# Two loads moved to a later place, x's differences on VectorE, and a front that begins two places later with its halves closer

## The chip, the cores and the metric

The kernel runs on one core of a Trainium2 chip. Its time is the device time of one launch, in microseconds (us), the median of three runs. A core has a matrix engine (TensorE, PE in the profile; its weight loads are PEld), VectorE (DVE), ScalarE (ACT), GpSimd (POOL) and SyncE (SP). Each engine works through its own instructions in order. SP only issues transfers (DMA) between the chip's memory (HBM) and the core's on-chip buffer, and it stands still at a transfer whose target is not yet free; ACT issues some transfers too.

## The reference

For each of 8 batches (8 heads, 576 positions, 64 channels a head), linear attention, then a perceptron on the normed rows, then an expert layer that needs the result:

```
q_s = softmax(q over channels);  k_s = softmax(k over positions)
x   = q_s @ (k_s^T @ v)                       # heads side by side: 576 x 512
xn  = (x - mean(x)) / sqrt(var(x) + 1e-6) * g_ln
x   = x + relu(xn @ w_ch1) @ w_ch2            # 512 -> 2048 -> 512
out = sum over each row's 2 best of 4 experts of weight * (causal attention of the expert)(x)
```

All numbers are float32. The kernel splits an operand into a high and a low part for the matrix engine and multiplies three of the four combinations, so each product is three matmuls.

## The kernel before, in words

The work of this case lies in the first half of the program, which makes x of every batch and runs 12 of the 16 column blocks of the perceptron (the rest and the experts come after about 760 us).

**Fronts.** `front(b)` is all that makes batch b ready for its perceptron: four *units* (`a_unit`, one for each pair of heads; unit n is pair n % 4 of batch n // 4), then the norm of the two halves of 288 rows (`layer_norm`), then the differences (`Mix`). A unit takes its k and q from tiles loaded for it; in its fourth piece it issues the loads of k and q for unit n + 2 (`load_qk(next_unit(n))`), and in its sixth those of v (`load_v`). The pools have two buffers, so unit n + 2 takes the buffers of unit n, and its load on SP waits until unit n has read them.

**Differences.** From batch 2 (`FAST`) on, the first product of the perceptron is done by a scheme with 7 products in place of 8: x's four quarters b11, b12, b21, b22 (column half, row half) and four differences t1 to t4 of them, each 128 x 576. `Mix.less` makes a difference; `Mix.part` splits a quarter or a difference into high and low (ACT, then DVE, the helper on lines 201 and 202). In the trace the differences are line 777 (`sq<-xc` is t1, `sq<-xc,sq` t2, `xc<-xc` t3, `xc<-xc,sq` t4), the split quarters `xm` and `xw_b`, the split differences `xw_a`.

**Rounds.** Batches 2 to 7 have a round each, `fast_pieces(b)`. A round is a list of TensorE pieces, by groups: 7 products of 2 x 6 matmuls (`fast_group`; they write banks pa, pb, pc), then 8 sums of 12 matmuls (`second`; acc), each of which DVE adds to x (L1418) before its bank is used again. The weights of a product come as one 512 KB tile `w_r`, streamed from HBM into five tiles in turn (`Stream`): the load of tile n is issued in the program right after product n - 5 has freed it. The fifth of the five exists only from `last_space` on, which stands after the first pieces of batch 2's round.

**Places.** `run_pieces` divides a round's matmuls into 44 places (`END`) and puts the steps of the next batch's front between them: unit pr begins at place 4 * pr (`UNIT_GAP`), the norm's halves `NORM_GAP` places apart, the differences behind. All of it is moved forward by `EARLY` places, so that a front's first steps fall into the round before. Batch 2's own front has no such move; it lies in the last pass of the simple method.

**What sets the order.** Program order decides on SP. On the other engines a scheduler reorders within the program's dependences by a timeline of its own, so a changed place also moves instructions around it. The order below is read from the built programs.

Of the kernel before, what the change touches and what calls it, by code (L numbers as in the profile page):

```python
# [12 lines left out]
ALU = mybir.AluOpType  # L13
# [27 lines left out]


UNIT_AT, UNIT_GAP = (0, 1, 2, 4, 5, 7), 4
NORM_AT, NORM_GAP = (0, 2, 4, 6, 8, 10), 8

REBASE = 2.0 ** -112

# [3 lines left out]
FAST = 2  # L51
# [89 lines left out]
def tile_kernel(ctx: ExitStack, tc: tile.TileContext, q, k, v, g_ln, w1, w2, w_gate, wq, wk, wv, wo, out):  # L141
    nc = tc.nc
# [5 lines left out]
    NPR = H // 2  # L148
# [48 lines left out]
    def pool(name, bufs=1, **kw):  # L197
        return tc.tile_pool(name=name, bufs=bufs, reuse_waits="tile", **kw)
# [34 lines left out]
    def x_hl(pl, name):  # L233
        return pl.tile([P, 2, NDC, T], F32R, tag="big", name=name)


    class Wide:
# [7 lines left out]
        def load(self):  # L245
            n = len(self.tiles)
            if n < len(self.blocks):
                r = self.pool_r.tile([P, DM, 2], I32, tag="r", name="wraw")
                src = self.blocks[n][0]
                dst = r.rearrange("p f t -> p (f t)")  # L250
                if len(src.shape) == 3:
                    dst = dst.rearrange("p (c f) -> p c f", c=src.shape[1])
                nc.sync.dma_start(out=dst, in_=src)
                self.tiles.append(r)
# [70 lines left out]
    def fc_tiles(pl, f, w=None):  # L325
        w1s[f] = pl.tile([P, 2, NDC, P], F32R, tag=f"w1_{f}", name=f"w1_{f}") if w is None else w
        w2s[f] = pl.tile([P, 2, DM], F32R, tag=f"w2_{f}", name=f"w2_{f}")
        return fc_blocks(f, w1s[f], w2s[f])
# [54 lines left out]
    def unit_buf(n):  # L383
        return n if n < NPR else n % 2

    def next_unit(n):

        return n + NPR if n < 2 else n + 2 if n >= NPR else len(units)
# [4 lines left out]
    def load_qk(n):  # L393
        for nm in "kq":
            load(n, nm)
# [13 lines left out]
    def load_v(n):  # L409
        if n >= len(units):  # L410
            return
        b, pr = units[n]
        t = vbuf[unit_buf(n)]
        base = v[b, 2 * pr]
        rows = lambda first, dims: bass.AP(tensor=base.tensor, offset=base.offset + first * D, ap=dims)
        for j in range(2):
            nc.sync.dma_start(out=t[:CS, :NIL, j, :D],
                              in_=rows(j * S, [[NIL * D, CS], [D, NIL], [1, D]]))
        nc.sync.dma_start(out=t[:, NIL, :, :D],
                          in_=rows(S - P, [[D, P], [S * D, 2], [1, D]]))  # L420
# [184 lines left out]
    def a_unit(n):  # L605

        u = Heads(n)
        for piece in (u.k_rows, u.q_max, u.q_below):
            piece()
        yield  # L610
        for piece in (u.k_turn, u.k_max, u.q_exp):
            piece()
        yield
        for piece in (u.k_spread, u.k_below, u.k_exp, u.q_sum, u.q_more, u.q_one, lambda: u.q_scale(0), lambda: u.q_scale(1)):
            piece()
        yield
        if next_unit(n) >= 2 * NPR:
            load_qk(next_unit(n))
        u.q_turn()
        for piece in u.q_parts(0):  # L620
            piece()
        yield
        u.kv_product()
        for piece in u.q_parts(1):
            piece()
        u.kv_sums()
        for j in range(2):
            u.kv_high(j)
            u.kv_low(j)
        yield  # L630
        if next_unit(n) >= 2 * NPR:
            load_v(next_unit(n))
        for h in range(NH):
            u.result(h)
            u.keep(h)
        yield
# [5 lines left out]
    class Norm:  # L642
# [40 lines left out]
        def less(self, c, n):  # L683
            if c == 0:
                self.xc = lp.tile([P, NDC, T], F32, tag="xc", name="xc", bufs=2)
            nc.vector.tensor_tensor(self.xc[:, c:c + n], self.xs[:, c:c + n],
                                    self.pmu[:, None].to_broadcast([P, n, T]), op=ALU.subtract)
# [75 lines left out]
    class Mix:  # L763
# [10 lines left out]
                self.at["t1"], self.at["t2"] = u.sq[:, :2], u.sq[:, 2:]  # L774

        def less(self, o, x, y):
            nc.gpsimd.tensor_tensor(self.at[o], self.at[x], self.at[y], op=ALU.subtract)

        def early(self):
            self.less("t1", "b12", "b11")  # L780
# [120 lines left out]
    def calls(fn):  # L901
        while True:
            fn()
            yield
# [11 lines left out]
    def load_wqk(s, r):  # L916
        def fill(t):
            for j in range(2):
                nc.sync.dma_start(out=t[:, :, j * D:(j + 1) * D],
                                  in_=(wq, wk)[s][2 * r + j].rearrange("(c p) d -> p c d", p=P))  # L920
        w = wqk[s, r] = mid.tile([P, 2, NDC, P], F32R, tag="r", name="wqk")
        load_moe(hp, fill, w[:, 0], w[:, 1])

    def load_wv(r):
        def fill(t):
            for j in range(2):
                nc.sync.dma_start(out=t[:, :, j * D:(j + 1) * D],
                                  in_=wv[2 * r + j].rearrange("(c p) d -> p c d", p=P))
        w = moe["vg"]
        load_moe(hp, fill, *(w[:, i, :, r * P:(r + 1) * P] for i in (0, 1)))  # L930
# [336 lines left out]
    def cut(t, at, shape):  # L1267
        n = 1
        for d in shape[1:]:
            n *= d  # L1270
        t = t[:, at:at + n]
        if len(shape) == 4:
            t = t.rearrange("p (a b c) -> p a b c", a=shape[1], b=shape[2])
        elif len(shape) == 5:
            t = t.rearrange("p (a b c d) -> p a b c d", a=shape[1], b=shape[2], c=shape[3])
        else:
            t = t.rearrange("p (a b) -> p a b", a=shape[1])
        return t
# [190 lines left out]
    def once(fn):  # L1469
        fn()  # L1470
        yield
# [9 lines left out]
        yield  # L1481

    late = ExitStack()
    END, EARLY = 44, 4

    def front(b):
        slots = front_slots(b)
        mixes[b] = m = Mix(b)
        add = lambda n, fn: slots.setdefault(n, []).append(once(fn))
        t = max(slots) + 1  # L1490
        add(t, m.early)
        if b == FAST:
            for i, nm in enumerate(("b11", "b21")):
                add(t - 6 + i, lambda nm=nm: m.part(nm))
            add(t + 2, m.fourth)
            add(t + 2, m.send)
            add(48, lambda: x_pair(("b12", "b22")))
            for i, nm in enumerate(("b12", "b22", "t1", "t2", "t3")):
                add(49 + i, lambda nm=nm: m.part(nm))
        else:  # L1500
            add(t + 0.5, lambda: m.part("b12"))
            for i, nm in enumerate(XMADE):
                add(t + 1 + i / 2, lambda nm=nm: m.part(nm))
            add(t + 4.5, m.send)
            slots = {n - EARLY: gs for n, gs in slots.items()}
        return slots

    slots = front(FAST)
    fronts = {FAST + 1: front(FAST + 1)}
    def begin(b, slots, end):  # L1510

        for n in [n for n in fronts.get(b, ()) if n < 0]:
            slots.setdefault(end + n, []).extend(fronts[b].pop(n))
# [21 lines left out]
    for b in range(FAST, B):  # L1535
        if b < LAST:
            slots, n = fronts.pop(b + 1), END
            if b + 2 < B:
                fronts[b + 2] = front(b + 2)
                begin(b + 2, slots, n)  # L1540
        else:
            slots, n = {}, 4 * NFC
            p1r.close()
            x2s_last[0] = t = x_hl(xtp, "x2")
            t = t.rearrange("p a b c -> p (a b c)")
            stream.use(before_last + 7, before_last + 7 * NG, [cut(t, 8 * P * i, WSL) for i in range(2)] + ring[MIDB:] +
                       [later[2].tile(WSL, F32R, tag="qT", name="w_r")])
            wcp = late.enter_context(pool("w_c", side="right"))
            moe["vg"] = wcp.tile([P, 2, NDC, VG], F32R, name="wvg")
            blocks = []  # L1550
            for f in range(FSPLIT, NFC):
                blocks += fc_tiles(wcp, f)
            wide = Wide(blocks, mid, hp, AHEAD)
            conv = calls(wide.step)
            todo = [conv] * len(blocks)
            for s in range(2):
                for r in range(NR):
                    todo.append(calls(lambda s=s, r=r: load_wqk(s, r)))
            for r in range(NR):
                todo.append(calls(lambda r=r: load_wv(r)))  # L1560
            todo.append(calls(load_g))
            for i, g in enumerate(todo):
                slots.setdefault(8 + 2 * i, []).append(g)
        pieces = fast_pieces(b)
        run_pieces(pieces, slots, n)
# [559 lines left out]
```

## Time and profile before

| | |
|---|---|
| median of 3 runs | 1339.03 us (1337.44 to 1343.73) |
| the profiled execution | 1340.05 us, span 1338.3 us |
| busy: PE / DVE / ACT / POOL | 1292.9 / 979.9 / 734.2 / 403.2 us |
| mean granted TensorE clock | 0.994 of full speed |
| end of batch 2's round, of batch 3's round | about 336 us, 424 us |

The span is the time from the first instruction to the last; the rest of an execution's time lies around it. PE is busy for 97% of the span: 45 us of it are idle, and about 30 of these lie between 200 and 760 us, in the rounds. A wait of PE costs its own length, and more if the granted clock falls after it.

### The profile page before, as it was taken

The page shows a single profiled execution, that of the slowest core. Times are in us where ns is not written, and L with a number is a line of the kernel's source. Part 1 is how long each engine was busy: PE and PEld are TensorE (multiplying, and loading weights), DVE is VectorE, ACT ScalarE, POOL GpSimd, SP SyncE. Part 2 cuts the span into 40 slices and gives each one's busy share as a digit, 9 for nine tenths or more (in the row PEclk, how much of TensorE's full clock was granted, in tenths as well). Part 3 has the DMA queues.
Part 4 walks back from the last instruction along what each step waited for, and adds up shares of the span by engine and source line. Part 5 has one row for each costly group of instructions (what it writes and reads, how often), then busy time and mean ns, then how long its engine had stood idle before and what let it go on. Part 6 is the DMA issues. An engine that isn't in the chain of part 4 may idle for free.

```text
span 1338.3 us, 27463 instructions
## 1 busy us (share of the span) xinstructions
PE 1292.9 (97%) x9919; PEld 1242.6 (93%) x9919; DVE 979.9 (73%) x2770; ACT 734.2 (55%) x1878; POOL 403.2 (30%) x496
## 2 busy tenths in 40 slices
PE   6999999979999999999998999999999999999998
PEld 5789999979998998989998999999999999999996
DVE  6985676968878787796667357777777777777774
ACT  6875444544545454445536235656566666665665
POOL 6676335443233332332215002122121112121222
PEclk9999999989999999999999999999999999999999
DMA  9763375666757758565557133333323232333122
GB/s 239 230 215 105 124 241 174 222 183 217 204 155 263 216 184 259 157 218 168 179 201 245 56 85 121 101 98 82 109 81 115 70 102 94 96 103 91 45 50 74
DMA packets 172406, 199.85 MB, mean 149 GB/s; under 512 B 93040, under 2 KB 137584, under 8 KB 169968
## 3 DMA queue, kind: packets, MB, share of 16 engines
q1 hardware_dynamic: 149648, 161.13, 41.0%
q10 hardware_dynamic: 22624, 36.97, 7.7%
q8 instruction: 79, 1.29, 0.4%
q14 instruction: 55, 0.45, 0.1%
HBM read 136.46 MB, written 46.40 MB: 137 GB/s over the span
## 4 chain that ended last, share of the span: by engine, by line
PE 72%; DVE 11%; DMA 5%; ACT 2%; issue 2%; POOL 1%; SPq 1%; ACTq 0%; DVEq 0%; POOLq 0%
PE acc L192 14%; PE psh L192 12%; PE psqk L192 7%; PE psc L192 7%; PE pa L195 6%; PE pssc L192 4%; PE pso L192 4%; PE py L192 4%; PE psv L192 4%; PE pc L195 3%; PE pst L1874 3%; DMA k<-in_k_dram 1%; PE po L192 1%; DMA q<-in_q_dram 1%; PE pb L195 1%
## 5 line engine op out<-in xcount | busy, mean ns | idle before, releaser
L192 PE MATMUL psh<-xhl,w 128*128 128x288 f32 x1248 | 188.6, 298 | 1.3 <-DVE xhl L717 1.0
L192 PEld LDWEIGHTS psh<-xhl,w 128*128 128x128 f32 x1248 | 172.2, 188 | 4.0 <-DVE xhl L717 1.5
L1857 POOL TENSOR_SCALAR sm<-sm,st,lg 128x128 f32<-128x128 f32 (+3 forms) x128 | 82.5, 655 | 265.4 <-DVE lg L1774 63.3
L192 PE MATMUL acc<-xw_a,w 128*128 128x288 f32 x948 | 136.8, 297 | 6.3 <-DVE xT L1418 4.6
L192 PEld LDWEIGHTS acc<-xw_a,w 128*128 128x128 f32 x948 | 128.7, 188 | 8.3 <-DVE xT L1418 6.3
L192 PE MATMUL acc<-hid,w 128*128 128x288 f32 x864 | 122.3, 298 | 1.7 <-DVE tmp L1360 1.7
L192 PEld LDWEIGHTS acc<-hid,w 128*128 128x128 f32 x864 | 116.8, 188 | 2.7 <-issue 1.9
L192 PE MATMUL psqk<-x,wqk 128*128 128x288 f32 x768 | 112.9, 297 | 0.4 <-DVE k L1677 0.4
L192 PEld LDWEIGHTS psqk<-x,wqk 128*128 128x128 f32 x768 | 105.1, 188 | 1.6 <-PE pst L1874 0.6
L192 PE MATMUL psc<-hb,w 128*128 128x288 f32 x672 | 100.2, 298 | 0.0
L1845 ACT ACTIVATE sm<-sm,st 128x128 f32<-128x128 f32 (+3 forms) x144 | 83.9, 584 | 21.0 <-DVE st L1837 19.4
L192 PE MATMUL acc<-hh,w 128*128 128x288 f32 x588 | 91.7, 300 | 2.9 <-DVE hh L826 1.5
L192 PEld LDWEIGHTS psc<-hb,w 128*128 128x128 f32 x672 | 92.1, 188 | 0.3
L1418 DVE TENSOR_TENSOR xT<-xT,acc 128x288 f32<-128x288 f32 x152 | 66.5, 446 | 33.0 <-PE acc L192 32.5
L192 PEld LDWEIGHTS acc<-hh,w 128*128 128x128 f32 x588 | 81.6, 188 | 6.3 <-DVE hh L826 3.0
L1898 ACT ACTIVATE aTh<-pst 128x128 fp32r<-128x128 f32 (+4 forms) x224 | 70.2, 333 | 23.3 <-PE pst L1874 10.7
L1899 DVE TENSOR_TENSOR aTl<-pst,aTh 128x384 fp32r<-128x384 f32 (+3 forms) x196 | 72.4, 381 | 11.4 <-ACT aTh L1898 9.1
L1837 DVE CUSTOM_DVE_ANT_0 sm<-pssc,mask 128x128 f32<-128x128 f32 (+2 forms) x144 | 67.9, 482 | 16.3 <-PE pssc L192 7.0
L195 PE MATMUL pa<-xw_a,w_r 128*128 128x288 f32 x384 | 63.7, 309 | 8.3 <-DMA w_r<-w_d 7.3
L661 POOL TENSOR_TENSOR sq<-sq 128x288 f32<-128x288 f32 x42 | 38.2, 910 | 105.6 <-ACT sq L692 103.6
L515 POOL TENSOR_TENSOR qe<-q,sm 128x320 f32<-128x320 f32 x64 | 47.9, 767 | 73.2 <-PE pq L553 44.0
L461 POOL TENSOR_TENSOR q<-q,sm 128x640 f32<-128x640 f32 x32 | 42.4, 1328 | 81.7 <-DVE sm L458 81.6
(255 smaller groups left out, 3117.4 us busy)
## 6 DMA issues: line engine op xcount, KB each, us to landing
w_r<-w_d SPq DMA_DIRECT2D x111, 512.0 KB, 5.0
wraw<-in_moe_w_ch_dram SPq DMA_DIRECT2D x32, 512.0 KB, 4.7
xhl<-xn_d SPq DMA_DIRECT2D x14, 1152.0 KB, 5.0
xp_d<-xT ACTq DMA_DIRECT2D x16, 576.0 KB, 4.1
xn_d<-xm ACTq DMA_DIRECT2D x16, 576.0 KB, 6.2
k<-k SPq DMA_DIRECT2D x32, 288.0 KB, 3.9
k<-in_k_dram SPq DMA_DIRECT2D x32, 256.0 KB, 3.8
q<-in_q_dram SPq DMA_DIRECT2D x32, 256.0 KB, 4.1
```

The source lines that it names most:

```text
L192: nc.tensor.matmul(o, lhsT, rhs, start=start, stop=stop)
L195: nc.tensor.matmul(o, lhsT, rhs, start=start, stop=stop, skip_group_check=True)
L461: nc.gpsimd.tensor_tensor(self.q3, self.q3, self.sm[:, 0, :, None].to_broadcast([P, 2 * NCH, D]), op=ALU.subtract)
L515: nc.gpsimd.tensor_tensor(self.qe[:, :, j, :], self.qt[:, j], self.sm[:, 2, j * NCH:(j + 1) * NCH, None].to_broadcast([P, NCH, D]), op=ALU ...
L661: nc.gpsimd.tensor_tensor(self.t, self.t, self.sq[:, c], op=ALU.add)
L1418: nc.vector.tensor_tensor(xs[:, c], xs[:, c], ps, op=ALU.add)
L1837: nc.vector.tensor_tensor_reduce(out=sm[:m, c0:c1], in0=o_, in1=msk, scale=1.0, scalar=3e38 if n == 0 else st[:m, j, 0:1], op0=ALU.add, op ...
L1845: nc.scalar.activation(sm[:m, :w], sm[:m, :w], AF.Exp, bias=st[:m, j, last:last + 1], scale=-1.0, accum_out=st[:m, j, 2:3])
L1857: nc.gpsimd.tensor_scalar(sm[:m, :w], sm[:m, :w], st[:m, j, 3:4], self.gate()[:, j:j + 1], op0=ALU.mult, op1=ALU.mult)
L1874: nc.tensor.transpose(pt[:kw, kb * m:kb * m + m], sm[:m, kb * P:kb * P + kw], ident[:m, :m])
L1898: nc.scalar.activation(oh, from_, AF.Copy)
L1899: nc.vector.tensor_tensor(ol, from_, raw(oh), op=ALU.subtract)
```

## The change

Five edits. The loads of units 16 and 17 (batch 4) are no longer issued by units 14 and 15 (batch 3, `later_on`) but at places 24 and 28 of batch 2's round. `less` runs on VectorE instead of GpSimd. `EARLY` goes from 4 to 2, so each front from batch 3 on begins two places later. `NORM_GAP` goes from 8 to 6, so the second half of the norm begins two places closer to the first; with both, the second half and the differences stay at their places from batch 3 on (in batch 2's front they come two places earlier).

```
-NORM_AT, NORM_GAP = (0, 2, 4, 6, 8, 10), 8
+NORM_AT, NORM_GAP = (0, 2, 4, 6, 8, 10), 6
...
-        if next_unit(n) >= 2 * NPR:
+        later_on = u.b == FAST + 1 and u.pr >= NPR - 2
+        if next_unit(n) >= 2 * NPR and not later_on:
             load_qk(next_unit(n))
...
-        if next_unit(n) >= 2 * NPR:
+        if next_unit(n) >= 2 * NPR and not later_on:
             load_v(next_unit(n))
...
         def less(self, o, x, y):
-            nc.gpsimd.tensor_tensor(self.at[o], self.at[x], self.at[y], op=ALU.subtract)
+            nc.vector.tensor_tensor(self.at[o], self.at[x], self.at[y], op=ALU.subtract)
...
-    END, EARLY = 44, 4
+    END, EARLY = 44, 2
...
+            if b == FAST:
+                for i in range(2):
+                    n2 = (FAST + 2) * NPR + i
+                    slots.setdefault(24 + 4 * i, []).append(once(lambda n2=n2: (load_qk(n2), load_v(n2))))
```

SP before, in batch 2's round, from the loads of unit 16 on (k16 is k of unit 16; v0 is a buffer of v; w_r_3564 is the fifth weight tile):

```order
L404 DMA k16_3417<-in_k_dram 128x2x256
L406 DMA k16_3417<-in_k_dram 128x2x64
L404 DMA q16_3420<-in_q_dram 128x2x256
L406 DMA q16_3420<-in_q_dram 128x2x64
L417 DMA v0_136<-in_v_dram 112x4x64 x2
L419 DMA v0_136<-in_v_dram 128x2x64
L404 DMA k17_3544<-in_k_dram 128x2x256
L406 DMA k17_3544<-in_k_dram 128x2x64
L404 DMA q17_3547<-in_q_dram 128x2x256
L406 DMA q17_3547<-in_q_dram 128x2x64
L1328 DMA w_r_3564<-w_d_1963 128x1024
```

SP now, at the same part, from unit 15's v on (w_r_3531 is the fifth weight tile, w_r_3178 to w_r_3181 are the other four, loaded again):

```order
L417 DMA v1_140<-in_v_dram 112x4x64 x2
L419 DMA v1_140<-in_v_dram 128x2x64
L1329 DMA w_r_3531<-w_d_1963 128x1024
L1329 DMA w_r_3178<-w_d_1963 128x1024
L1329 DMA w_r_3179<-w_d_1963 128x1024
L1329 DMA w_r_3180<-w_d_1963 128x1024
L1329 DMA w_r_3181<-w_d_1963 128x1024
L1329 DMA w_r_3531<-w_d_1963 128x1024
L1329 DMA w_r_3178<-w_d_1963 128x1024
L1329 DMA w_r_3179<-w_d_1963 128x1024
L404 DMA k16_3825<-in_k_dram 128x2x256
L406 DMA k16_3825<-in_k_dram 128x2x64
```

The fifth weight tile now stands right behind unit 15's v, and the loads of unit 16 stand behind eight weight tiles.

VectorE before, at the end of batch 3's round (`xT<-xT,acc` is the add of one sum, `xm`, `xw_b` and `xw_a` are low parts of quarters and differences):

```order
L708 SCALAR_TENSOR_TENSOR xc<-xc,g_sb,pvar 128x288 x4
L202 TENSOR_TENSOR xm<-xc,xm 128x576
L314 SCALAR_TENSOR_TENSOR xw_a<-pa,xw_a 128x288
L314 SCALAR_TENSOR_TENSOR xw_a<-tmp,xw_a 128x288
L1418 TENSOR_TENSOR xT<-xT,acc 128x288
L202 TENSOR_TENSOR xw_b<-xc,xw_b 128x576
L202 TENSOR_TENSOR xm<-xc,xm 128x576
L202 TENSOR_TENSOR xw_a<-sq,xw_a 128x576
L1418 TENSOR_TENSOR xT<-xT,acc 128x288 x2
L202 TENSOR_TENSOR xw_a<-sq,xw_a 128x576
L477 TENSOR_REDUCE cm_5394<-pkm_5392 128x1
L454 TENSOR_REDUCE km_5487<-k_5327 128x128
```

VectorE now, at the same part (L778 are the differences):

```order
L709 SCALAR_TENSOR_TENSOR xc<-xc,g_sb,pvar 128x288 x4
L1419 TENSOR_TENSOR xT<-xT,acc 128x288
L778 TENSOR_TENSOR sq<-xc 128x576
L202 TENSOR_TENSOR xw_b<-xc,xw_b 128x576
L1419 TENSOR_TENSOR xT<-xT,acc 128x288
L202 TENSOR_TENSOR xm<-xc,xm 128x576
L778 TENSOR_TENSOR sq<-xc,sq 128x576
L778 TENSOR_TENSOR xc<-xc 128x576
L1419 TENSOR_TENSOR xT<-xT,acc 128x288
L202 TENSOR_TENSOR xw_a<-sq,xw_a 128x576
L1419 TENSOR_TENSOR xT<-xT,acc 128x288
L778 TENSOR_TENSOR xc<-xc,sq 128x576
```

Four differences stand among the low parts and the adds, and the unit's step (`km<-k`) is gone from this stretch.

PE before, in batch 2's round, from the last products of the second group to its first sum (`pvar` is the matmul of a half's variance, the second one here ends the norm's second half):

```order
L195 MATMUL pb<-xm,w_r 128x288 x6
L192 MATMUL pvar<-lnsum,mean_r 128x288
L553 MATMUL pq_4255<-ident,qe_4217 128x112 x4
L195 MATMUL pa<-xm,w_r 128x288 x6
L192 MATMUL pkv_4293<-v_136,ke_4212 64x66
L192 MATMUL pvar<-lnsum,mean_r 128x288
L192 MATMUL pkv_4293<-v_136,ke_4212 64x66 x2
L195 MATMUL pb<-xm,w_r 128x288 x6
L195 MATMUL pa<-xm,w_r 128x288 x6
L192 MATMUL acc<-hid,w_4_157 128x288 x3
```

PE now, at the same part:

```order
L195 MATMUL pb<-xm,w_r 128x288 x12
L195 MATMUL pa<-xm,w_r 128x288 x12
L192 MATMUL pvar<-lnsum,mean_r 128x288
L553 MATMUL pq_4296<-ident,qe_4246 128x112 x4
L192 MATMUL pkv_4326<-v_136,ke_4241 64x66 x10
L192 MATMUL acc<-hid,w_4_157 128x288 x3
L192 MATMUL acc<-hid,w_6_593 128x288 x3
L192 MATMUL acc<-hid,w_5_158 128x288
L192 MATMUL pvar<-lnsum,mean_r 128x288
L192 MATMUL acc<-hid,w_5_158 128x288 x2
```

The second pvar has moved from among the products into the first of the eight sums, with 7 of the 96 matmuls of the sums before it.

## Rows read from the trace of the kernel before

**Rows 1.** PE's waits: for what, total us, times, longest.

```profile
PE pa L195 <- DMA w_r<-w_d: 8.8, 3, 7.3
PE acc L192 <- DVE xT L1418: 4.6, 6, 0.9
...
PE pc L195 <- DVE xT L1418: 2.1, 2, 1.1
```

**Rows 2.** Stretches: length, PE, PEld, DVE, ACT, POOL busy (instructions), granted clock, DMA share, GB/s.

```profile
280.00:290.00 10.00, 3.18 (x13) 3.18 (x14) 4.47 (x11) 3.06 (x8) 4.32 (x5) 0.62 1.01 293
290.00:300.00 10.00, 10.00 (x68) 10.00 (x67) 6.87 (x16) 4.88 (x11) 3.38 (x4) 0.87 0.65 216
...
410.00:420.00 10.00, 9.32 (x75) 8.85 (x74) 10.00 (x13) 3.60 (x6) 5.99 (x4) 1.00 0.84 296
```

**Rows 3.** PE's timeline in batch 2's round: start, us, instruction, [idle before].

```profile
271.36 2.00 PE L195 MATMUL pa<-xm,w_r 128*128 128x288 f32 x12
...
278.74 0.80 PE L192 MATMUL pkv<-v,ke 112*64 112x66 f32 x20
286.82 1.09 PE L195 MATMUL pa<-xw_a,w_r 128*128 128x288 f32 x3 [7.28 <-DMA w_r<-w_d]
287.70 1.16 PE L192 MATMUL po<-qT,kv 128*128 128x288 f32 x4
288.67 2.36 PE L195 MATMUL pa<-xw_a,w_r 128*128 128x288 f32 x9
290.82 0.68 PE L192 MATMUL po<-qT,kv 128*128 128x288 f32 x2
291.31 2.37 PE L195 MATMUL pb<-xm,w_r 128*128 128x288 f32 x12
...
296.58 5.36 PE L192 MATMUL acc<-hid,w 128*128 128x288 f32 x39
```

**Rows 4.** SP's timeline in the same stretch: issue, us of issuing, transfer.

```profile
265.31 0.57 SPq L419 DMA_DIRECT2D v<-in_v_dram  x1
...
278.71 0.37 SPq L404 DMA_DIRECT2D k<-in_k_dram  x1
...
280.91 0.46 SPq L1328 DMA_DIRECT2D w_r<-w_d  x1
```

**Rows 5.** Weight tiles loaded from 240 to 345 us: issue to landing.

```profile
DMA to landing us min/median/max: 3.4/5.9/9.8
```

**Rows 6.** The differences on POOL: ns min/median/max, first and last start.

```profile
L777 POOL TENSOR_TENSOR sq<-xc x6: 1431/1438/1443, 247.2 to 671.7; 128x576 f32<-128x576 f32 x6
L777 POOL TENSOR_TENSOR sq<-xc,sq x6: 1527/1828/1957, 249.8 to 673.2; 128x576 f32<-128x576 f32 x6
```

**Rows 7.** Low parts of the same size on DVE, 340 to 690 us: ns min/median/max.

```profile
L202 DVE TENSOR_TENSOR xm<-xc,xm x16: 745/756/1840, 398.2 to 681.7; 128x576 fp32r<-128x576 f32 x16
...
L202 DVE TENSOR_TENSOR xw_a<-sq,xw_a x8: 744/1364/1995, 415.5 to 679.6; 128x576 fp32r<-128x576 f32 x8
```

**Rows 8.** Chain of waits, end of batch 2's round: start, us, what.

```profile
319.53 0.33 PE pvar L192
...
324.46 1.70 DVE xc L708 x4
...
329.44 1.63 DVE xw_a L202
...
334.33 1.59 DVE xw_a L202
335.92 0.38 DVE xT L1418
...
336.34 1.06 PE pa L195 x6
```

**Rows 9.** PE's timeline at the end of batch 3's round.

```profile
417.88 3.44 PE L192 MATMUL acc<-xw_a,w 128*128 128x288 f32 x24 [0.68 <-DVE xT L1418]
...
422.33 1.87 PE L192 MATMUL acc<-xw_a,w 128*128 128x288 f32 x12 [0.90 <-DVE xT L1418]
```

## The prediction

> **What bounds the kernel now.** I read the page first: PE is busy almost throughout, so the change can pay only where PE waits or runs at a lower clock. Second, PE's waits [rows 1]: in the rounds the largest is for a weight tile (8.8 us in 3 times, one of them 7.3 us), then come waits for VectorE's adds, 4.6 us and 2.1 us in sum, of at most about a microsecond each. Third, the stretches of 10 us [rows 2]: from 280 to 290 us PE is busy 3.18 us and the granted clock is 0.62, from 290 to 300 us it is 0.87, a mean between the two levels (1.2 and 2.4 GHz); elsewhere in the rounds it is at or near 1.00. Fourth, the timelines of PE and SP there. PE ends unit 15's pkv at 278.74 + 0.80 = 279.54 and then waits 7.28 us for the fifth tile [rows 3]. SP issued that tile at 280.91, after k17 at 278.71 [rows 4], which stands ahead of it in the queue and waits for unit 15 to free its buffer. So the tile is not slow; it is issued late. Issue to start of the product is 286.82 - 280.91 = 5.9 us, the median landing of such tiles [rows 5]. Last, the chain of waits at the round's end [rows 8]: from 320 to 336 us it runs over VectorE, though PE shows only small waits there. The two are nearly level in that stretch.
>
> **The change, part by part.** *The later loads.* They move 7 issues each of units 16 and 17 (2 for k, 2 for q, 3 for v), 14 in all; unit 16's now stand behind eight weight tiles. The fifth tile is then next after unit 15's v. That v is issued by 265.31 + 0.57 = 265.9 us now [rows 4]; a front that begins two places later (a round's 88 us over 44 places is 2 us a place) can push it to 270 us. With the median landing of 5.9 us the tile is there at 276 us, with the longest of 9.8 us at 279.7 us [rows 5]. PE wants it at 279.5 us. So the wait of 7.28 us goes.
>
> With it goes the slow clock behind it. From 286.82 us to the end of pb at 293.68 us PE does 3 + 4 + 9 + 2 + 12 = 30 matmuls in 6.9 us; at the later pace of 5.36/39 = 0.137 us [rows 3] they take 4.1 us. That is 2.7 us more. Together -10.0 us.
>
> What is late next: the sixth tile, which takes the first tile's place. Its product ends at 271.36 + 2.00 = 273.4 us; the load lands at 279.3 us, or at the longest at 283.2 us. PE wants it 12 matmuls after 279.5 us, at 281.1 us. That is a wait of 0 to 2.1 us; I take +0.7, near the median.
>
> The loads moved back have their price on VectorE: the first step of unit 16 (km16) would stand waiting in VectorE's queue if k16 came late, and behind it the adds that free PE's banks. PE has four banks of 12 matmuls (1.65 us each), 6.6 us of cover against a landing a few us after the round's first seven products. I take 0 here; with the longest landing the cover is nearly used up and the cost about 1 us.
>
> *The differences on VectorE.* 4 in each of 6 fronts, 24 in all. On POOL one takes 1.44 us with POOL's neighbours quiet and 1.83 us at the median of the second form [rows 6]. On VectorE the trace has none; the nearest rows are low parts of the same size and type of operation: 0.75 us at the shortest, 2.0 us at the longest [rows 7]. I take 0.75, since the long ones are those beside POOL's differences, which go. So VectorE gets 4 x 0.75 = 3.0 us a front, or 8 us at the longest. It loses part of that: the split differences have a median of 1.36 us against 0.75, and in the chain of waits two of them took 1.6 us [rows 8]; five of them at some 0.7 less each (0.6 to 0.9 by these rows) are 3.5 us a front. Net about 0, from -3.5 to +8 us of VectorE's time. How much reaches PE: at 410 to 420 us VectorE is busy all 10.00 us [rows 2], and there PE waits 0.68 and 0.90 us for adds [rows 9]. So VectorE has no cover left at a round's end.
>
> On this the Trainium skill, "SBUF — State Buffer", section "Who interferes with whom", says that a VectorE instruction with two inputs in the on-chip buffer contends with a GpSimd instruction that reads it, and that the loser is blocked for the whole instruction. The trace agrees as far as 0.75 against 2.0 us goes. By the rule the moved differences, which have two such inputs, can themselves be blocked by what stays on POOL, which speaks against the change; it would carry them towards the 2.0 us of the row, and the sum below towards the first rival.
>
> *EARLY and NORM_GAP.* Nothing is added. The four units and the norm's first half move two places back; the second half stays. In the order, unit steps leave VectorE's list at the round's end, where the differences come in. The price is a tighter chain: from the second half's pvar to the next round's first product there are 336.34 - 319.53 = 16.8 us today [rows 8]; in the new order pvar stands in the first of the last eight sums, so 96 - 7 = 89 matmuls or 12.2 us are left. VectorE's work between is four differences and five low parts at 0.75 us, the scaling at 1.70 and eight adds at 0.38 [rows 7, 8], 11.5 us, and it starts late, after pvar has gone through ACT. The next round's first products need neither the last adds nor the later differences, which gives some 2 us back. So the ends come out even: per round between -1.6 us (today's waits go) and +2 us. I take -1 us over all rounds, between -6.7 (all waits for adds) and +18 (24 x 0.75, nothing hidden).
>
> **Sum.** -10.0 + 0.7 - 1 = -10.3 us. From the profiled execution's 1340.05 us that gives 1329.8 us. That execution is 1.0 us above the median of the runs, 1339.03 us; for the median I say 1329 us, 0.75% less. About 0.5%, or 6.7 us, is what a measurement of this kernel can tell from no change: 1332.3 us and 1345.7 us are the bounds.
>
> **The rivals.**
> First, slower: VectorE becomes the bound at each round's end. It is full there already [rows 2], and each round's first products need the differences. If none of the 3.0 us hides, six fronts cost 18 us, and 1339.0 - 10.0 + 18 = 1347 us. It decides from 10.0/6 = 1.7 us a front on. Against it: POOL's differences slow VectorE today [rows 7], and that goes.
> Second, part of the gain is given back at the ends of the rounds. The chain over VectorE of 16.8 us against 12.2 us left costs 4.6 us in batch 2's round, where the stall gave it time, and little in the later ones: 1339 - 9.3 + 4.6 = 1334 us. For it speaks that the chain runs over VectorE at 320 to 336 us [rows 8]; against it, that the chain itself loses POOL's share.
> Third, the stall does not go but moves to the sixth tile: with the longest landing PE waits 2.1 us, and if that too brings the clock down for 2.7 us, 1339 - 10.0 + 4.8 = 1334 us. For it: the transfers are dense there (DMA share 1.01 in 280 to 290 us [rows 2]), though without the bunched loads they should be less so.
> Fourth, better: besides the stall all waits for adds go (6.7 us [rows 1]): 1339 - 10.0 - 6.7 = 1322 us.
>
> **How the numbers follow.** Forecast 0.55, first rival 0.09, second 0.15, third 0.08, fourth 0.13. The forecast's own range is 1325 to 1333 us; the range for 8 in 10 takes in the fourth rival in part and the second and third: 1321 to 1338 us. The first rival lies outside with its 0.09. Faster by over 0.5% (below 1332.3 us): the forecast and the fourth, 0.68, and a little of the others, 0.70; slower: 0.09; within: 0.21.
>
> **What would show it.** In the changed kernel's profile the wait of pa for w_r near 280 us is gone or under 1 us, and the granted clock is 1.00 in every stretch from 250 to 310 us; SP issues the fifth tile before 271 us. The differences are on VectorE at 0.75 to 0.9 us, and the low parts xw_a have a median near 0.75 us. PE's waits for adds at the rounds' ends are between 0 and 2 us a round. It would be wrong if PE waits for a split difference or for pvar in each round, if VectorE waits for k16, or if a tile other than the fifth brings a wait of several us.

## The result, and the profile after

The changed kernel takes 1327.35 us (median of 6 runs, 1323.8 to 1330.1), the kernel before 1338.42 us on the same chip (6 runs, 1336.64 to 1343.73): a ratio of 0.9908 [0.989, 0.9926], or 11 us less. Its profiled execution took 1329.71 us, with a span of 1328.0 us against 1338.3. The forecast was 1329 us; for the profiled execution its sum said 1329.8 us.

The sum holds, but two of its terms don't. PE's timelines give the marks for this, the first psh of batch 2 and the first product of rounds 3 and 7, in us of the span:

```
stretch                          before          after           change
start to batch 2's first psh     234.6           238.4            +3.8
batch 2's round                  100.3            94.4            -5.9
rounds 3 to 6                    348.2           340.5            -7.7
round 7 to the end               655.2           654.6            -0.6
span                            1338.3          1328.0           -10.3
```

The +3.8 us of the first row are not the change's alone: the kernel of the first experiment has the same instructions as before up to there and reached that mark at 237.9 us. And in the changed kernel 8 matmuls of the pass before, about 1.1 us, come ahead of that mark that came behind it before, so 1.1 us of the +3.8 and of the -5.9 are only that move.

**The stall is gone.** The timeline of SP in the changed kernel (issue, us of issuing, transfer) answers to [rows 4]:

```profile
267.87 0.57 SPq L419 DMA_DIRECT2D v<-in_v_dram  x1
268.49 19.43 SPq L1329 DMA_DIRECT2D w_r<-w_d  x8
287.97 0.43 SPq L404 DMA_DIRECT2D k<-in_k_dram  x1
```

The fifth tile is issued from 268.49 us on, right behind unit 15's v, and unit 16's k only at 287.97 us. The tiles loaded from 240 to 345 us land sooner than in [rows 5]:

```profile
DMA to landing us min/median/max: 3.3/4.5/6.8
```

The stretches of 10 us (columns as in [rows 2]):

```profile
280.00:290.00 10.00, 10.00 (x92) 9.77 (x91) 7.26 (x21) 6.59 (x18) 1.70 (x3) 1.00 0.76 250
290.00:300.00 10.00, 10.00 (x77) 10.00 (x76) 6.31 (x11) 2.09 (x5) 2.94 (x4) 1.00 0.97 235
...
310.00:320.00 10.00, 7.57 (x59) 6.93 (x58) 10.00 (x24) 6.78 (x14) 3.15 (x5) 0.83 0.59 192
...
403.00:413.00 10.00, 10.00 (x79) 9.77 (x78) 9.96 (x22) 4.88 (x10) 0.00 (x0) 1.00 0.69 254
```

Where PE did 3.18 us of work at a granted clock of 0.62 it now does 10.00 at 1.00. Batch 3's round ends 6.9 us sooner than before (417.16 us against 424.06), so 403 to 413 us answers to the 410 to 420 us of [rows 2]. PE is full there now. VectorE is nearly as full as before (9.96 us), but it gets through 22 instructions where it had 13. The new loss is from 310 to 320 us: PE 7.57, VectorE 10.00, clock 0.83. In the kernel before that stretch reads:

```profile
310.00:320.00 10.00, 10.00 (x79) 9.61 (x77) 9.31 (x18) 7.78 (x19) 4.29 (x5) 1.00 0.73 245
```

PE's timeline there in the changed kernel, from the first product after the eight sums (301.23 us):

```profile
301.23 1.49 PE L195 MATMUL pa<-xm,w_r 128*128 128x288 f32 x10
...
309.06 1.76 PE L195 MATMUL pa<-xw_a,w_r 128*128 128x288 f32 x12
310.66 0.27 PE L486 MATMUL pkm<-ident,cm 128*128 128x128 f32 x1
311.69 0.30 PE L559 MATMUL pkv<-ident,qe 128*128 128x128 f32 x1 [0.75 <-DVE xc L687]
313.66 2.97 PE L195 MATMUL pb<-xm,w_r 128*128 128x288 f32 x12 [1.67 <-DVE tmp L1361]
316.42 1.83 PE L195 MATMUL pa<-xm,w_r 128*128 128x288 f32 x9
```

and VectorE's, which shows why the adds of `tmp` are late:

```profile
308.92 1.30 DVE L454 TENSOR_REDUCE km<-k 128x128 f32<-128x640 f32 x1
310.13 1.41 DVE L687 TENSOR_TENSOR xc<-xT,pmu 128x576 f32<-128x576 f32 x2
311.46 1.78 DVE L709 SCALAR_TENSOR_TENSOR xc<-xc,g_sb,pvar 128x288 f32<-128x288 f32 x4
313.16 0.81 DVE L1361 TENSOR_TENSOR tmp<-pc,tmp 128x288 f32<-128x288 f32 x2
```

A unit's step (`km`), the subtraction of the mean in the norm's second half (L687) and the scaling of its first half (L709), 4.5 us back to back, stand ahead of the adds that free PE's banks. In the kernel before, the timelines of PE and of VectorE have the same marks, the first product after the sums, the scaling and the first of the adds:

```profile
308.43 0.29 PE L195 MATMUL pa<-xm,w_r 128*128 128x288 f32 x1
```

```profile
308.11 1.79 DVE L708 SCALAR_TENSOR_TENSOR xc<-xc,g_sb,pvar 128x288 f32<-128x288 f32 x4
...
314.63 0.46 DVE L1360 TENSOR_TENSOR tmp<-pc,tmp 128x288 f32<-128x288 f32 x1 [0.69 <-PE pkv L559]
```

So PE comes 7.2 us sooner to these products, but the scaling comes 3.4 us later: it began 0.3 us ahead of them and now begins 10.2 us behind them. Of the 3.4 us 2.7 are order, since the scaling stood ahead of the other two steps and now stands behind them. The adds come 1.5 us sooner (313.16 us against 314.63): before, VectorE waited 0.69 us for PE there, and now PE waits for VectorE. PE pays 0.75 + 1.67 us of waits, and the slower clock behind them costs pb 2.97 - 1.76 = 1.2 us and the nine of pa 1.83 - 9 x 1.76/12 = 0.5 us: 4.1 us together.

**VectorE.** The differences (first two of four lines; ns min/median/max) and the low parts from 340 to 690 us, which answer to [rows 6, 7]:

```profile
L778 DVE TENSOR_TENSOR sq<-xc x6: 736/750/755, 250.9 to 665.4; 128x576 f32<-128x576 f32 x6
L778 DVE TENSOR_TENSOR sq<-xc,sq x6: 748/750/1384, 254.1 to 667.7; 128x576 f32<-128x576 f32 x6
```

```profile
L202 DVE TENSOR_TENSOR xm<-xc,xm x16: 744/750/1274, 395.4 to 673.2; 128x576 fp32r<-128x576 f32 x16
L202 DVE TENSOR_TENSOR xw_a<-sq,xw_a x8: 747/748/752, 412.7 to 671.1; 128x576 fp32r<-128x576 f32 x8
```

The low parts of differences fell from 1364 to 748 ns at the median and from 1995 to 752 at the longest.

**PE's waits** from 240 to 690 us (total us, times, longest) answer to [rows 1]:

```profile
PE pa L195 <- ACT tmp L1353: 2.8, 1, 2.8
PE pb L195 <- DVE tmp L1361: 1.7, 1, 1.7
PE pa L195 <- DMA w_r<-w_d: 0.8, 1, 0.8
```

From 260 us on no wait for the adds of xT is left. The first line is new, and though it names ACT it begins with a load. The timeline of the engines there, from VectorE to PE:

```profile
456.95 0.82 DVE L458 TENSOR_REDUCE sm<-q 128x10 f32<-128x640 f32 x1 [4.54 <-DMA q<-in_q_dram]
...
459.05 0.17 DVE L577 RECIPROCAL ks<-ks 128x2 f32<-128x2 f32 x1
459.25 0.31 ACT L582 ACTIVATE kv<-pkv,ks 64x64 fp32r<-64x64 f32 x1 [4.87 <-DVE ks L577]
459.46 0.39 ACT L1353 ACTIVATE tmp<-pa 128x288 f32<-128x288 f32 x1
...
459.90 1.10 PE L195 MATMUL pa<-xw_a,w_r 128*128 128x288 f32 x6 [2.78 <-ACT tmp L1353]
```

VectorE stands 4.54 us at a step that needs q; ks stands behind it, ACT's kv waits for ks, the copy of `tmp` stands behind kv, and PE waits for that copy. No one of the four is slow.

### The profile page after: what moved, and what is told of

Its sections match the earlier page's. It is cut to its first block, busy times and chain, and to the rows that moved or that the text cites. A ratio compares the mean times of both kernels' runs of the same rounds, so it can differ in the third digit from the quotient of the medians.

```text
span 1328.0 us, 27448 instructions
## 1 busy us (share of the span) xinstructions
PE 1292.5 (97%) x9919; PEld 1242.2 (94%) x9919; DVE 971.7 (73%) x2794; ACT 734.3 (55%) x1878; POOL 360.2 (27%) x472
## 5 line engine op out<-in xcount | busy, mean ns | idle before, releaser
L461 POOL TENSOR_TENSOR q<-q,sm 128x640 f32<-128x640 f32 x32 | 43.1, 1347 | 155.2 <-DVE sm L458 151.6
L195 PE MATMUL pa<-xw_a,w_r 128*128 128x288 f32 x384 | 59.2, 298 | 4.1 <-ACT tmp L1353 4.1
L662 POOL TENSOR_TENSOR sq<-sq 128x288 f32<-128x288 f32 x42 | 36.2, 862 | 99.3 <-ACT sq L693 97.1
```

Of the source, the lines that this page charges most:

```text
L195: nc.tensor.matmul(o, lhsT, rhs, start=start, stop=stop, skip_group_check=True)
L461: nc.gpsimd.tensor_tensor(self.q3, self.q3, self.sm[:, 0, :, None].to_broadcast([P, 2 * NCH, D]), op=ALU.subtract)
L662: nc.gpsimd.tensor_tensor(self.t, self.t, self.sq[:, c], op=ALU.add)
```

## The experiments

Each ratio is to runs of the kernel before on the same chip; a saving in us is what the ratio leaves off 1340 us. The first six are parts of the change.

**Later loads alone.** Only these lines of the change are applied:

```
+ later_on = u.b == FAST + 1 and u.pr >= NPR - 2
+ ... and not later_on:   (for load_qk and load_v)
+ slots.setdefault(24 + 4 * i, []).append(once(... load_qk(n2), load_v(n2)))
```

> Before, with only the two late loads (fronts, halves and GpSimd's differences as before). Theory (the queue: the fifth weight tile was late because it stood behind unit 17's loads): the 7.28 us wait of pa for w_r and the 2.7 us of slow clock go, 8 to 11 us faster, ratio 0.992 to 0.994, and the waits for adds at the rounds' ends (0.7 and 0.9 us) stay. Rival A (give-back: the end of batch 2's round is bound by VectorE beside GpSimd's differences, so without the relief the time returns there): 3 to 6 us faster, with PE waits of 4 us or more between 310 and 330 us. Rival B (it is the relief of VectorE that pays): within 2 us of before.

Measured: 1335.71 against 1341.15 us, 0.996 [0.9944, 0.9975], 5.4 us saved. The stall is gone, but PE's timeline has the new waits too:

```profile
312.90 0.30 PE L559 MATMUL pkv<-ident,qe 128*128 128x128 f32 x1 [0.64 <-DVE xc L687]
315.41 1.81 PE L195 MATMUL pb<-xm,w_r 128*128 128x288 f32 x6 [2.08 <-DVE tmp L1361]
```

So the new waits come with the loads, not with the differences, which stayed on GpSimd here. Half of the 10 us arrives: rival A's time, with new waits of 2.7 us where it named 4 or more.

**All but the loads** (the same lines left out, the rest of the change applied).

> The changed kernel with the loads of units 16 and 17 issued where the units issue them. The later places put unit 16's k and q ahead of the fifth weight tile and unit 17's k, q ahead of the sixth. Theory (queue): the stall moves to the sixth tile and stays at 4 us or more with the slow clock behind it; ratio to before 0.995 to 1.000, 4 to 10 us slower than the changed kernel. Rival B (VectorE's relief pays): ratio 0.991 to 0.994, as the changed kernel.

Measured: 1329.46 against 1341.15 us, 0.991 [0.9892, 0.9928], 12.1 us saved. That is rival B's ratio, and the whole change's, without the part that was to bring nearly all of it. SP's timeline shows what became of the stall:

```profile
274.08 0.46 SPq L1329 DMA_DIRECT2D w_r<-w_d  x1
...
282.28 0.46 SPq L406 DMA_DIRECT2D q<-in_q_dram  x1
282.83 0.42 SPq L1329 DMA_DIRECT2D w_r<-w_d  x1
```

The two place numbers also move the weight tiles among the loads: the fifth tile now goes out behind unit 16's k and q, at 274.08 us, and the sixth behind unit 17's, at 282.83. PE's only wait for a tile in that round is for the sixth:

```profile
287.41 2.25 PE L195 MATMUL pb<-xm,w_r 128*128 128x288 f32 x12 [2.59 <-DMA w_r<-w_d]
```

**Differences alone.**

```
- nc.gpsimd.tensor_tensor(... op=ALU.subtract)
+ nc.vector.tensor_tensor(... op=ALU.subtract)
```

> Before, with only x's differences on VectorE. Theory: the stall of 7.28 us stays; the low parts fall to 0.75 us, the waits for adds at the rounds' ends shrink by 0 to 1.5 us a round: 0 to 5 us faster, ratio 0.996 to 1.000. Rival (VectorE pays the differences): 3 to 18 us slower, ratio 1.002 to 1.013, with longer waits for adds. Rival B (the relief pays): 8 to 11 us faster.

Measured: 1337.39 against 1341.15 us, 0.9978 [0.9965, 0.9991], 2.9 us saved. The stall stays, later than before:

```profile
294.63 1.09 PE L195 MATMUL pa<-xw_a,w_r 128*128 128x288 f32 x3 [6.71 <-DMA w_r<-w_d]
```

Batch 2's round takes 108.1 us against 100.3, and rounds 3 to 6 take 337.1 against 348.2. So the move pays in the rounds' ends and costs in batch 2's round, where PE also waits 5.1 us in three times for `cm` of a unit, 2.44 us at the longest. The ratio is the theory's.

**No differences** (loads and places, `less` left on GpSimd).

> The changed kernel with the differences back on GpSimd. Theory (queue pays, the rest small): 0 to 5 us slower than the changed kernel, ratio to before 0.991 to 0.995. Rival A (the closer front needs the relief): the front's end, in 12 us where 17 us stood, is too tight with differences of 1.4 to 1.9 us on GpSimd; 5 to 15 us slower than the changed kernel, PE waits for split differences at the rounds' starts. Rival B (the relief pays everything): as before, ratio 0.998 to 1.002.

Measured: 1331.96 against 1341.15 us, 0.9939 [0.9916, 0.9963], 8.2 us saved. Low parts on VectorE and differences on POOL from 340 to 690 us:

```profile
L202 DVE TENSOR_TENSOR xm<-xc,xm x16: 744/978/1624, 396.1 to 672.1; 128x576 fp32r<-128x576 f32 x16
L202 DVE TENSOR_TENSOR xw_a<-sq,xw_a x8: 1618/1798/1981, 412.7 to 669.2; 128x576 fp32r<-128x576 f32 x8
L202 DVE TENSOR_TENSOR xw_b<-xc,xw_b x4: 1087/1100/1104, 409.8 to 664.0; 128x576 fp32r<-128x576 f32 x4
```

```profile
L778 POOL TENSOR_TENSOR xc<-xc,sq x4: 1945/1945/1950, 414.0 to 668.2; 128x576 f32<-128x576 f32 x4
```

With the differences beside them the eight low parts of the second line take 1798 ns at the median, without them (the changed kernel) 748. The ratio is the theory's. Rival A falls: PE does not wait for split differences in rounds 3 to 6.

**Places alone** (EARLY 2, NORM_GAP 6).

> Before, with EARLY 2 and NORM_GAP 6 alone. The runs so far have rounds 3 to 6 at 348 us before, 337 us with places and differences, 337 us with differences alone, 342 us with places and loads, 350 us with loads alone. Theory now (two separate gains: the queue in batch 2's round, which places or later loads give alike, and VectorE's relief at the ends of rounds 3 to 6, which places or differences give): batch 2's round ends 3 to 5 us earlier with a wait of 2 to 3 us for the sixth tile, rounds 3 to 6 take 340 to 343 us; ratio 0.992 to 0.996. Rival (places need the later loads or the differences with them): the stall or waits for the differences stay, ratio 0.997 or more.

Measured: 1337.26 against 1340.62 us, 0.9977 [0.9968, 0.9987], 3.1 us saved: the rival's ratio. The stall moves to the sixth tile and shrinks:

```profile
292.77 3.25 PE L195 MATMUL pb<-xm,w_r 128*128 128x288 f32 x12 [4.67 <-DMA w_r<-w_d]
```

**Loads and differences** (places as before).

> The changed kernel with EARLY 4 and NORM_GAP 8, so later loads and differences on VectorE without the moved places. Theory (two separate gains): the stall goes by the loads, rounds 3 to 6 take 336 to 339 us by the differences; the differences cost batch 2's own front 3 us or more, since VectorE is full there; ratio to before 0.991 to 0.995. Rival (the places are what pays): 0.996 or more.

Measured: 1333.48 against 1340.62 us, 0.9943 [0.9927, 0.996], 7.6 us saved. That is the theory's ratio, but rounds 3 to 6 took 347.8 us and not its 336 to 339. Round 3 starts with these waits of PE:

```profile
336.45 0.85 PE L195 MATMUL pa<-xw_a,w_r 128*128 128x288 f32 x2 [2.45 <-ACT xw_a L201]
...
338.86 2.77 PE L195 MATMUL pc<-xw_a,w_r 128*128 128x288 f32 x10 [1.56 <-DVE xw_a L202]
```

Both are for split differences, which come late there with the old places; 1.04 us for `cm` of a unit stand ahead of them.

All three together save 12.3 us by the same reckoning. Differences and places bring 6 us more together than apart; the loads bring 5 us by themselves and 0.2 on top of the other two. The intervals are some 2 us to either side. The marks of the result's table, of one profiled execution each, show where (a wait at round 3's first products counts in rounds 3 to 6):

```
us                        batch 2's round   rounds 3 to 6   saved, by ratio
before                         100.3            348.2             -
loads                           96.2            349.9            5.4
differences                    108.1            337.1            2.9
places                         100.0            343.3            3.1
loads, differences              92.7            347.8            7.6
loads, places                   93.2            341.6            8.2
differences, places             97.1            336.9           12.1
all three                       94.4            340.5           12.3
```

**Fronts as early as before, norms closer** (the changed kernel with EARLY 4). This order writes quarters of x before the last products that read them, so those products use other values; the work is the same.

> The changed kernel with EARLY 4, so the second half of the norm and the differences come two places earlier than in either kernel. Theory: what pays at the rounds' ends is that VectorE's steps are spread; with more time behind the front the ends stay free of waits, 0 to 3 us slower than the changed kernel: ratio 0.990 to 0.994. Rival (the two places back are what clears the ends): waits for adds of 1.5 us a round come back, ratio 0.995 or more.

Measured: 1323.2 against 1340.62 us, 0.9876 [0.9862, 0.989]; rounds 3 to 6 took 335.5 us. That is faster than the theory said, and the rival's waits for adds did not come back (0.5 us in all in rounds 3 to 6).

**Norm halves eight apart** (the changed kernel with NORM_GAP 8).

> The changed kernel with NORM_GAP 8, so the second half of the norm and the differences come two places later than in either kernel. Theory (the front's end is level with VectorE's work, about 12 us left): two places or 4 us less make it late, PE waits 1 to 4 us for split differences at each round's start, ratio 0.995 to 1.005. Rival (there is room): ratio 0.990 to 0.993.

Measured: 1329.14 against 1340.62 us, 0.9921 [0.9905, 0.9938]: no difference from the changed kernel that can be told, as the rival said.

**Early fronts, mixing held back** (EARLY 4, `m.part` and `m.send` two places later).

> The changed kernel, with fronts begun four places early as in the kernel before, their norms still six places apart, and the mixing step with its sending held back two places, so that the quarters are written where they are now. Theory 'the starts of rounds want a front that ends early' (e7 had rounds 3 to 6 in 335.5 us against 340.5 for the changed kernel): most of e7's 5 us come again, ratio to the kernel before 0.988, rounds 3 to 6 in 336 to 338 us. Rival 'what e7 gained came from the quarters written earlier': the held version gives nothing over the changed kernel, ratio 0.991, rounds 3 to 6 in 340 us or more.

Measured: 1331.41 against 1342.86 us, 0.9911 [0.9892, 0.9929]; rounds 3 to 6 took 344.5 us. The rival holds: what the early front gained came with the quarters written early, which the buffers don't allow.

**Half way: EARLY 3, NORM_GAP 7.**

> The changed kernel with places half way between the old and the new: fronts three places early, norms seven apart. Theory 'the two place numbers act together and each half step costs half': ratio between e4-like and changed kernel, 0.991 to 0.993. Rival 'the places matter little once VectorE makes the differences and only single waits move': 0.991 plus or minus 0.001 with rounds 3 to 6 between 337 and 341 us, as with e8 (norms eight apart, 338.1 us).

Measured: 1330.55 against 1342.86 us, 0.9909 [0.9893, 0.9926]; rounds 3 to 6 took 345.4 us, longer than the rival said, and batch 2's round 91.0 us, shorter. The total doesn't move.

**Batch 2's own differences on GpSimd, the others on VectorE.**

```
- nc.vector.tensor_tensor(...)
+ (nc.gpsimd if self.b == FAST else nc.vector).tensor_tensor(...)
```

> The changed kernel with the differences of batch 2's own front on GpSimd as before and those of the other fronts on VectorE. Theory 'VectorE is the bound only in batch 2's round, and there the differences are an added load, while in rounds 3 to 6 they pay': batch 2's round as in e4 (93 to 94.5 us) and rounds 3 to 6 as in the changed kernel (about 340 us) or better: ratio 0.990 to 0.991. Rival 'the slower differences of that front push it back': its round begins later and the time is over 1329 us, ratio 0.992 or more.

Measured: 1324.66 against 1342.86 us, 0.9857 [0.9837, 0.9878], below what the theory and the rival said and below the changed kernel's interval: a version that beats both, by some 0.5% against the changed one (through the kernel before; the two did not run side by side). Its marks are as the theory said, batch 2's round 93.7 us and rounds 3 to 6 338.2 us, both a little shorter than in the changed kernel. The wait for VectorE's adds stays nearly as it was in PE's timeline:

```profile
314.71 1.07 PE L195 MATMUL pb<-xm,w_r 128*128 128x288 f32 x6 [1.68 <-DVE tmp L1361]
```

but the granted clock does not fall behind it, nor at 460 to 470 us, where the changed kernel has 0.83:

```profile
310.00:320.00 10.00, 7.78 (x71) 7.12 (x70) 10.00 (x20) 7.01 (x15) 4.88 (x5) 1.00 0.73 222
...
460.00:470.00 10.00, 10.00 (x77) 9.94 (x77) 8.10 (x22) 4.72 (x14) 1.56 (x2) 1.00 0.71 261
```

Its profiled execution is 5.1 us shorter, spread over all stretches. Why four differences on another engine bring that is open.

**The stall put back into the changed kernel.** k and q of units 16 and 17 go out ahead of the fifth tile again; everything else stays.

```
- slots.setdefault(24 + 4 * i, []).append(once(... (load_qk(n2), load_v(n2))))
+ slots.setdefault(12, []).append(once(... load_qk(n2)))
+ slots.setdefault(24 + 4 * i, []).append(once(... load_v(n2)))
```

> The changed kernel with the k and q loads of units 16 and 17 both put ahead of the fifth weight tile again, the v loads left late. The stall near 280 us should come back: the fifth tile issued at about 280 us behind k17 and q17, PE waiting 6 to 8 us for it at a lower granted clock behind it. Theory of the prediction (the stall costs 10 us on the path): 1337 us, ratio 0.998 to 0.999. Rival 'VectorE is nearly level there, so most of the stall is given back by waits that vanish at 311 to 316 us': 1327 to 1331 us, ratio 0.991 to 0.994, batch 2's round longer by at most 4 us and the waits for VectorE at 311.7 and 313.7 us gone or smaller.

Measured: 1332.11 against 1342.86 us, 0.9919 [0.9902, 0.9935]. The stretch from 280 to 290 us and PE's timeline show the stall:

```profile
280.00:290.00 10.00, 4.16 (x41) 3.45 (x40) 6.00 (x16) 5.56 (x14) 4.58 (x6) 0.94 0.64 193
```

```profile
282.49 0.80 PE L192 MATMUL po<-qT,kv 128*128 128x288 f32 x4 [1.73 <-ACT kv L582]
...
289.10 3.25 PE L195 MATMUL pa<-xw_a,w_r 128*128 128x288 f32 x12 [4.11 <-DMA w_r<-w_d]
...
314.65 0.96 PE L195 MATMUL pc<-xm,w_r 128*128 128x288 f32 x6
315.45 0.27 PE L559 MATMUL pkv<-ident,qe 128*128 128x128 f32 x1
```

PE loses 1.73 + 4.11 us to waits and 3.25 - 1.76 = 1.5 us to the clock, 7.3 us. But from 308 to 318 us it now waits for nothing, so the 4.1 us of the changed kernel are gone: 3.2 us should be left. Batch 2's round is 4.7 us longer (99.2), and the ratio is 0.0011 higher, 1.5 us. That 1.5 us lies within the intervals. The prediction's theory said a ratio of 0.998 to 0.999, the rival 0.991 to 0.994: the rival holds, with a round that is a little longer than its 4 us. The two times expected were those of the first chip; on this one the kernel before took 4.4 us more.

## Why the prediction was right in its sum and wrong in two of its terms

**The stall, -10.0 us: the wait went as said, the gain was over-sized.** The fifth tile is issued at 268.49 us, before the 271 us named, and the clock is 1.00 from 250 to 310 us. But batch 2's round is only 5.9 us shorter, and the loads alone save 5.4 us. The step that failed is the one on what is late next: I looked at the sixth tile and at k16, and not at VectorE's work for the norm. PE reaches the products behind the sums 7.2 us sooner; the norm's steps don't come sooner by as much, and the adds of those products stand behind them. That gives back 4.1 us, and -10.0 + 4.1 = -5.9. That this meets the measured -5.9 to the tenth is luck: the round's small waits changed too (1.76 us at 258.51 us and 0.37 went, five of 1.95 us in all came), and 1.1 us of the -5.9 are the 8 matmuls that moved ahead of the mark. The experiment that puts the stall back shows the exchange in the other direction: a stall of 7.3 us there, these waits gone, and a cost of 1.5 us (ratio) to 4.7 us (batch 2's round in the profile). The second rival had this mechanism, with 4.6 us, but placed it some 15 us later, at the round's end. That PE's and VectorE's chains are nearly level, as the prediction said of 320 to 336 us [rows 8], held for the stretch before as well: VectorE had only 0.69 us to spare ahead of the adds at 314.63 us.

**The sixth tile, +0.7 us: 0.** With landings of 6.8 us at the longest it brings no wait; the third rival falls in the changed kernel. It is real in the parts: 4.67 us with places alone, 2.59 with places and differences.

**k16, 0 us: not 0 in the trace.** The prediction named a VectorE that waits for k16 as a sign against it, and VectorE does wait. Behind that wait stands the subtraction of the mean in the norm's first half:

```profile
294.61 1.31 DVE L454 TENSOR_REDUCE km<-k 128x128 f32<-128x640 f32 x1 [2.84 <-DMA k<-in_k_dram]
...
297.29 1.41 DVE L687 TENSOR_TENSOR xc<-xT,pmu 128x576 f32<-128x576 f32 x2
```

In the kernel before it stands right behind the matmuls of the mean (`pmu`), which end at 296.74 us:

```profile
296.78 1.42 DVE L686 TENSOR_TENSOR xc<-xT,pmu 128x576 f32<-128x576 f32 x2 [0.58 <-PE pmu L192]
```

PE stays busy all of 290 to 300 us through it. But in the changed kernel `pmu` ends at 294.62 us, so the norm's chain goes on 2.7 us later than it could, and steps of that chain stand ahead of what PE waits for at 311 to 313 us. The late k16 is not the only cause: the kernel without the later loads has the wait for VectorE's adds too, in PE's timeline:

```profile
316.46 1.85 PE L195 MATMUL pb<-xm,w_r 128*128 128x288 f32 x12 [1.45 <-DVE tmp L1361]
```

How much of the 4.1 us is k16's no run separates.

**The differences, net 0 on VectorE: right.** 16 of them in rounds 3 to 6 cost 16 x 0.75 = 12 us. The low parts lose about as much: in the kernel with loads and places alone, by the medians of its forms, 8 x (1.80 - 0.75) and 4 x (1.10 - 0.75) and 16 x (0.98 - 0.75) make 13.5 us. On the rule that spoke against the move, the Trainium skill, "SBUF — State Buffer", section "Who interferes with whom" (a VectorE instruction with two inputs in the on-chip buffer contends with a GpSimd instruction that reads it): the trace agrees, with 1798 ns beside POOL's differences against 748 without them. Of the moved differences only the second form has an instruction as long as 1384 ns; in the other three none is over 755. So what stayed on POOL hardly meets them. The first rival (1347 us) falls: VectorE is nearly as full at the end of batch 3's round as before (9.96 us of 10), but with shorter instructions, 22 in place of 13, and no add of xT is late.

**The rounds' ends, -1 us: under-sized, -7.7 us measured in rounds 3 to 6**, outside the term's own -6.7 to +18. All waits for adds of xT went, as in the fourth rival; I had put it at 0.13, because I read a VectorE that is full as one without cover and not as one that is slowed. The price of the tighter chain, up to +2 us a round, did not come. The chain from the second half's `pvar` to the next round's first product is 12.0 us now, near the 12.2 said; before it was 15.4 us and not 16.8, since that product begins at 334.90 us and 336.34 us is its second part. PE's idle time in rounds 3 to 6 fell from 8.4 to 2.9 us; the other 2.1 us are shorter busy time, which I have not traced. (From 200 to 760 us PE was idle 24.0 us before, not about 30.) Either edit pays there alone: rounds 3 to 6 take 337.1 us with the differences alone and 343.3 with the places alone, against 348.2 before and 336.9 with both. (With the later loads the differences alone do little there, 347.8 us against 349.9, and PE waits up to 2.45 us for split differences.) What the two edits bring more together than apart lies in batch 2's round, 97.1 us with both against 108.1 and 100.0 with one: there both are 10.7 us better than the sum of the parts, in rounds 3 to 6 4.7 us worse. Some of that is the stall, which shrinks to 2.59 us with both (6.71 and 4.67 with one). The rest I have not traced further.

**A wait that no term had:** 2.78 us at 459.90 us, which the load of q brings about over VectorE's queue. It is part of the 340.5 us.

So the errors nearly cancelled: +4.1 us on the stall, -0.7 on the sixth tile, -6.7 on the rounds' ends, and +3.8 and -0.6 us ahead of and behind the rounds, where no term stood (3.3 of the 3.8 us came in the kernel with the loads alone too, where nothing had changed up to that mark). The time was right for reasons that were half right: the later loads, to which the prediction gave nearly all of the gain, are worth 0.2 us, not to be told from none, once the other two parts are there.

## What to carry to other kernels

Before a stall is booked as gain, ask what else it gave time to: follow the next 30 us of each engine's work, and see whether what the bound engine needs there comes sooner too. An engine that is busy for all of a stretch may be slowed by a neighbour and not full of work; the spread of one shape's duration (744 to 1995 ns here) tells which. Parts of a change that treat one wait are not to be added: time each alone and each left out.

## What the runs showed of the hardware

PE's clock fell behind quite short waits, and not always: after 0.75 and 1.67 us within 3 us the granted clock of 310 to 320 us was 0.83 in the changed kernel, after 0.54 and 1.68 us it was 1.00 in the mixed one. In the changed kernel these 2.4 us of waits cost 4.1 us with the slower clock.

The weight tiles loaded from 240 to 345 us, eight of them issued as one run, landed in 4.5 us at the median and 6.8 at the longest, against 5.9 and 9.8 us [rows 5] where they came among the bunched loads of k, q and v.
